# GpSimd's two-operand SBUF work on VectorE, and the float64 shift and weight casts on ScalarE, in a fused attention and mixture-of-experts kernel

## The chip, the cores and the metric

The kernel runs on one core of a Trainium2 chip. The metric is the device time of one execution in microseconds (us). The engines are TensorE (PE; its weight loads are a row of their own, PEld), VectorE (DVE), ScalarE (ACT), GpSimd (POOL) and SyncE (SP). Each engine works through its own queue of instructions in order and waits for other engines by semaphores. A line number such as L750 is a line of the kernel.

## The reference, cut to what matters

Three layers follow each other on 1536 tokens of 512 features. The weights of the middle one, `w_in` and `w_out`, are float64.

```python
# 1: attention, 2 batches x 8 heads, 768 tokens, 64 features: a window of 16 to both sides,
#    and the maxima (keys) and means (values) of each block of 32 tokens
a = softmax(concat([masked q.k / 8, q.kmax / 8 + log(32)]))
x = a @ concat([v, vmean])
# 2: a dense layer, 512 -> 2048 -> 512
h = x @ w_in
x = (h * sigmoid(h)) @ w_out
# 3: 8 experts, 512 -> 1024 -> 512, each token to the one with the largest logit
e = argmax(x @ w_gate);  p = softmax(x @ w_gate)[e]
out = p * (relu(x @ w1[e]) @ w2[e])
```

## The kernel before, in words

Matrix products are made at nearly float32 precision from three products of two parts. A matrix is split into a *high* part, a cast to the matmul type, and a *remainder*, the matrix less its high part. A high part is one copy, a remainder one subtraction of two operands. This splitting is most of what VectorE, ScalarE and GpSimd do.

The tokens go in six chunks of 256. For each chunk and each of four pairs of heads there are scores on PE (`dots`), minima on VectorE (`lows`, L331), exponentials on ScalarE (`exps`), their reciprocal sums on VectorE (`shares`), the normalisation on GpSimd (`norm`, L346), a transpose on PE (`turn`), its copy (`keep`), and the product with the values (`values`), split into `x_high` and `x_rest`. The dense layer goes in eight steps per chunk: `first` (PE, L389), `tanh` (ScalarE), `gated` (VectorE, L402, the scaled product for the sigmoid gate), `g_high` (mostly ScalarE), `g_rest` (mostly GpSimd, L410), and `second` (PE, L426), which runs two steps behind `first`.

The dense weights come as float64 words: 32 blocks of 128 x 512, read as pairs of 32-bit words, low and top. `shrink` (L229) scales the top word's exponent range. `join` shifts the low word down by 29 bits (L233) and joins the top word, moved up by three, to it (L234). `sign_in` (L238) puts the sign back. `high` and `rest` (L256) then split the block. A block's place in SBUF is freed by its remainder, and the next block's load waits for that place.

`route_dots` (L467) makes the router's logits on VectorE, 16 dot products and read-outs a chunk. `route_pick`, `route_rank` and `route_write` put each token into a table by its expert. `plan` and what follows it, chains of small VectorE operations, decide which experts' tiles are worked on in which unit. The first two units come from the first five chunks, the others from all six. A unit loads its expert's weights (SyncE), gathers its tokens (GpSimd's indirect DMA), splits the weights in 16 pieces of 128 x 512 (`split_high`, L151; `split_rest`, L750), and runs both layers (L794 and L819 for a pair of tiles, L831 and L854 for a single tile). `relu_high` and `relu_rest` (L807) split the hidden layer, `scale` and `write` put the result out. The raw weights have one place per half matrix, so the next unit's loads wait for this unit's remainders.

The order of the work is written out by hand up to the first two units. `STEPS` is a table of 1203 short names; each calls the next step of its kind, and so puts its instructions at the end of their engines' queues. A mark behind a name chooses the engine: `'` VectorE, `*` ScalarE, `_` GpSimd; without one the step's own default holds. In it `a` is `shrink`, `b` `join`, `c` `sign_in`, `h` `high`, `p` `rest`, `F` `first`, `t` `tanh`, `u` `gated`, `g` `g_high`, `w` `g_rest`, `G` `second`, `d0` to `d5` one dot product of a chunk, `N0` to `N5` `norm`, `1h` and `2h` `split_high` of the two layers, `1r` and `2r` `split_rest`. The units after that are ordered by `run`, where two strings of 16 letters, `HIGH` and `REST`, say which engine splits which piece: of a unit's 16 remainders ten are VectorE's and six GpSimd's, of its casts 14 ScalarE's and two VectorE's.

Of the kernel before, what the change touches and what calls it, by code (L numbers as in the profile page):

```python
# [13 lines left out]
I64 = mybir.dt.int64  # L14
AF = mybir.ActivationFunctionType
# [6 lines left out]
P = 128  # L22
# [14 lines left out]
G = 4  # L37
# [20 lines left out]
w G D2 G t h_ p b c' u l l l l T2 b a a E2 h g' p p w a_ b F c' t c' F h R2 N2 b u a g q2 l l w p b A2 c' c' b t h h G P2 G a' b l u p p a h C2 g V2 F
b c' c' c' h a h p w p b l q2 l c' t H2 h L2 p b u p h_ A2 F G a a g w l D2 l c' p h t p F F T2 l l u E2 b g' R2 c' N2 h b t w p a P2 t G c' u g a C2'
u w' b h a p' V2 g b c' w' G l l q2 H2 c' h h a L2 F p l t b u b g' p w G D2 c' F A2 T2 h a E2 a t c' b p G h' c' R2 p u h N2 l G p' g b w' c' h' P2  # L60
p' F C2 a b t V2 D2 u c' g H2 h G p T2 E2 a w b F R2 L2 c' N2 h t p G l l u a a g' b w P2 F C2' c' h p' b V2 t F H2 u c' L2 h g p w G t u g w j j J j
# [12 lines left out]
ga rh rr ym 1h 1h 1r yo yo 1h' 1r' 1r' 1h 1r' f1 z 2h 2h 2r' f f lt f f rh rr lc lt lc 1h ls ls ga ga ga ga st 1r' 1h' 1r 1h' 1h 1r z z 1r f1 2r'
# [9 lines left out]
def fused_kernel(ctx: ExitStack, tc, qw, kw, kt, vw, vr, vt, w_in, w_out, w_gate, w1, w2, masks, blocks, items, out):  # L84
# [95 lines left out]
    def block_sums(j):  # L180
        """Sums over the first batch's blocks, on the rows that follow a window's: a column of ones for each block."""
# [22 lines left out]
    def means(b):  # L204
        """The blocks' mean values, on the rows that follow a window's."""
# [20 lines left out]
    def shrink(kind, f, by=nc.scalar):  # L226
        """Float64 words to float32, in place: the exponent's range first, then the bits moved up by three."""
        top = words((kind, f))[1].bitcast(F32)
        (by.mul if by is nc.scalar else by.tensor_scalar_mul)(top, top, TINY)  # L229

    def join(*x):
        low, top = words(x)
        nc.vector.tensor_scalar(low, low, 29, None, op0=ALU.logical_shift_right)  # L233
        nc.vector.scalar_tensor_tensor(low, top, three[:, 0:1], low, op0=ALU.logical_shift_left, op1=ALU.bitwise_or)  # L234

    def sign_in(kind, f, by=nc.gpsimd):
        low, top = words((kind, f))
        by.scalar_tensor_tensor(low, top, sign[:, 0:1], low, op0=ALU.bitwise_and, op1=ALU.bitwise_or)  # L238
# [25 lines left out]
    def rooms(c):  # L264
        """All of a chunk's queries, values and weights, while the places of the dense layers are free."""
# [837 lines left out]
```

## Time and profile before

| | us |
|---|---|
| median of 3 runs | 612.42 |
| the three runs | 605.81, 612.42, 612.69 |
| the profiled execution: span from its first to its last instruction | 605.5 |
| the fastest run, which lies 0.3 us above that span, taken for the profiled execution's own time | 605.81 |
| mean granted TensorE clock of the profiled execution | 0.953 of full speed |

The profile is of one execution. Its view of the busy times says how long each engine had an instruction running, and the windows say the same by stretch, with the granted clock of TensorE as a share of its full speed. In the groups of instructions, two numbers follow the bar: the time in which the group ran, and the mean duration of one in nanoseconds; behind the next bar stands the time in which the engine had been idle just before them, and what ended that. In the view of one line, three durations are given: shortest, median and longest.

### The profile page before, as it was taken

The page shows a single profiled execution, that of the slowest core. Times are in us where ns is not written, and L with a number is a line of the kernel's source. Part 1 is how long each engine was busy: PE and PEld are TensorE (multiplying, and loading weights), DVE is VectorE, ACT ScalarE, POOL GpSimd, SP SyncE. Part 2 cuts the span into 40 slices and gives each one's busy share as a digit, 9 for nine tenths or more (in the row PEclk, how much of TensorE's full clock was granted, in tenths as well). Part 3 has the DMA queues.
Part 4 walks back from the last instruction along what each step waited for, and adds up shares of the span by engine and source line. Part 5 has one row for each costly group of instructions (what it writes and reads, how often), then busy time and mean ns, then how long its engine had stood idle before and what let it go on. Part 6 is the DMA issues. An engine that isn't in the chain of part 4 may idle for free. (4 is left out here: it accounts for less than half of the span.)

```text
span 605.5 us, 9930 instructions
## 1 busy us (share of the span) xinstructions
PE 542.1 (90%) x3554; PEld 467.9 (77%) x3554; DVE 474.4 (78%) x1018; ACT 242.1 (40%) x575; POOL 281.8 (47%) x240
## 2 busy tenths in 40 slices
PE   7878876999999999999899989977799999999883
PEld 3667756778987889788889968866699898988661
DVE  5799999998646788878774586799967487778982
ACT  5764334444324443333332111632243554455531
POOL 2556675453422134252424134894557572454541
PEclk9969988998999999999999999977989999999987
DMA  9996323503377233231210003700056562356540
GB/s 321 327 316 215 104 79 109 187 1 104 117 227 258 70 108 48 81 48 54 79 13 2 36 0 125 260 0 1 1 159 212 184 233 77 97 198 236 185 158 10
DMA packets 40937, 76.24 MB, mean 126 GB/s; under 512 B 3910, under 2 KB 14764, under 8 KB 40882
## 3 DMA queue, kind: packets, MB, share of 16 engines
q1 hardware_dynamic: 35954, 65.81, 34.6%
q0 software_dynamic: 2912, 6.33, 3.1%
q10 hardware_dynamic: 2016, 3.40, 1.6%
q8 instruction: 30, 0.49, 0.4%
q14 instruction: 25, 0.20, 0.1%
HBM read 82.50 MB, written 7.19 MB: 148 GB/s over the span
## 5 line engine op out<-in xcount | busy, mean ns | idle before, releaser
L389 PE MATMUL h<-x,wi 128*128 128x256 f32 x1152 | 151.2, 288 | 5.8 <-DVE t L402 5.1
L426 PE MATMUL x<-wo,g 128*128 128x512 f32 x576 | 148.2, 405 | 5.5 <-POOL g L410 2.2
L389 PEld LDWEIGHTS h<-x,wi 128*128 128x128 f32 x1152 | 144.6, 194 | 8.0 <-issue 4.9
L426 PEld LDWEIGHTS x<-wo,g 128*128 128x128 f32 x576 | 106.2, 191 | 31.6 <-POOL g L410 2.8
L750 POOL TENSOR_TENSOR sp<-r,sp 128x512 fp32r<-128x512 f32 x65 | 88.1, 1387 | 27.2 <-ACT sp L151 22.6
L467 DVE CUSTOM_DVE_ANT_0 dull<-row,gate 128x512 bf16<-128x512 f32 x96 | 92.5, 964 | 3.1 <-DMA gate<-w_gate 1.0
L750 DVE TENSOR_TENSOR sp<-r,sp 128x512 fp32r<-128x512 f32 x79 | 80.5, 1051 | 16.3 <-ACT sp L151 15.8
L410 POOL TENSOR_TENSOR g<-t,g 128x512 fp32r<-128x512 f32 x40 | 58.0, 1455 | 54.4 <-ACT g L151 38.1
L151 ACT CAST sp<-r 128x512 fp32r<-128x512 f32 x123 | 68.8, 624 | 35.4 <-DMA r<-w 16.2
L794 PE MATMUL jh<-xTT,sp 128*128 128x256 f32 x576 | 77.9, 293 | 3.6 <-DVE jT L807 3.6
L794 PEld LDWEIGHTS jh<-xTT,sp 128*128 128x128 f32 x576 | 76.4, 201 | 6.0 <-DVE jT L807 3.9
L819 PE MATMUL jy<-sp,jT 128*128 128x512 f32 x288 | 75.1, 409 | 0.0
L819 PEld LDWEIGHTS jy<-sp,jT 128*128 128x128 f32 x288 | 54.3, 196 | 11.2
L346 POOL TENSOR_TENSOR a<-a,m 128x480 f32<-128x480 f32 x24 | 26.0, 1085 | 71.0 <-DVE m L342 32.4
L337 ACT ACTIVATE a<-a,m 128x120 f32<-128x120 f32 x96 | 36.9, 387 | 54.8 <-DVE m L331 52.5
L399 ACT ACTIVATE t<-h 128x512 f32<-128x512 f32 x48 | 28.5, 596 | 74.7 <-PE h L389 58.0
L402 DVE SCALAR_TENSOR_TENSOR t<-t,h 128x512 f32<-128x512 f32 x48 | 32.7, 682 | 23.7 <-ACT t L399 23.4
L803 ACT ACTIVATE jT<-jh 128x512 fp32r<-128x512 f32 x24 | 14.4, 599 | 61.7 <-PE jh L794 50.1
L863 POOL DMA_INDIRECT out<-y,ids x15 | 16.1, 1074 | 46.4 <-DVE y L859 18.7
L151 ACT CAST g<-t 128x512 fp32r<-128x512 f32 x32 | 19.8, 622 | 35.8 <-DVE t L402 30.8
L513 POOL DMA_INDIRECT tbl<-tb,ix x12 | 14.2, 1180 | 39.5 <-DVE cum L508 16.9
L807 DVE SCALAR_TENSOR_TENSOR jT<-jh,jT 128x512 fp32r<-128x512 f32 x24 | 16.5, 687 | 19.3 <-ACT jT L803 19.3
(181 smaller groups left out, 705.7 us busy)
## 6 DMA issues: line engine op xcount, KB each, us to landing
r<-w SPq DMA_DIRECT2D x36, 1024.0 KB
rawi<-w_in SPq DMA_DIRECT2D x16, 512.0 KB
rawo<-w_out SPq DMA_DIRECT2D x16, 512.0 KB
q<-qw SPq DMA_DIRECT2D x24, 256.0 KB
v<-vw SPq DMA_DIRECT2D x24, 192.0 KB
k<-kw SPq DMA_DIRECT2D x16, 240.0 KB
kt<-kt SPq DMA_DIRECT2D x8, 416.0 KB
x2d<-row ACTq DMA_DIRECT2D x12, 256.0 KB
```

Source lines behind the costliest of these rows:

```text
L151: (nc.scalar.copy if by is nc.scalar else by.tensor_copy)(dst, src)
L337: nc.scalar.activation(a[:, t], a[:, t], AF.Exp, bias=m[:, 0, t:t + 1], scale=-1.0, accum_out=m[:, 1, t:t + 1])
L346: nc.gpsimd.tensor_tensor(a, a, m[:, 2].unsqueeze(2).to_broadcast([P, G, NC]), op=ALU.mult)
L389: nc.tensor.matmul(hs[c, p][:, j], wi[p][:, u, k, j * P:(j + 1) * P], xt[c, k][:, v], start=(j + k + n == 0), stop=(j == 1 and k == KB - 1 ...
L399: nc.scalar.activation(t, hs[c, p], AF.Tanh, scale=0.5)
L402: nc.vector.scalar_tensor_tensor(ts[c, p], ts[c, p], 1.0, hs.pop((c, p)), op0=ALU.add, op1=ALU.mult)
L410: by.tensor_tensor(g[:, 1], ts.pop((c, p)), g[:, 0].bitcast(F32), op=ALU.subtract)
L426: nc.tensor.matmul(x2p[c][i], g[:, v, j, i * P:(i + 1) * P], wo[f][:, u], start=(f == 0 and n == 0), stop=(f == FB - 1 and n == 2))
L467: nc.vector.tensor_tensor_reduce(dull, r, gates[e], 1.0, 0.0, ALU.mult, ALU.add, lg[:, i * E + e:i * E + e + 1])
L750: by.tensor_tensor(dst[:, 1], src, dst[:, 0].bitcast(F32), op=ALU.subtract)
L794: nc.tensor.matmul(hps[i, p][:, j], sp1[p // 2 * 4 + k][:, u, f:f + P], x[v][:, k], start=(k + n == 0), stop=(k == 3 and n == 2))
L819: nc.tensor.matmul(yps[i, t], h[:, v, j, t * P:(t + 1) * P], sp2[2 * p + j][:, u], start=(p + j + n == 0), stop=(p == 3 and j == 1 and n = ...
```

## The change

Five parts:

- `norm`, `rest`, `g_rest` and `split_rest`, all of them operations on two SBUF operands, go from GpSimd to VectorE throughout; so does `sign_in`'s default. The marks in `STEPS` that moved single ones of them to VectorE, or from VectorE and GpSimd elsewhere, go.
- The shift of the low word leaves `join`, on VectorE, for `shrink`, on ScalarE. It reads the upper 16-bit half of the low word, scales it by 2^-13 with an offset that makes the conversion to a whole number round down, and writes 32-bit words.
- `shrink` is always ScalarE's: four were GpSimd's and two VectorE's.
- `high` is always ScalarE's: five were VectorE's or GpSimd's. Three `g_high` of GpSimd go to ScalarE; those of VectorE stay.
- In `run`, all casts go to ScalarE and all remainders to VectorE. The eight casts that `STEPS` marks for VectorE (`1h'`, `2h'`) stay there.

```diff
-    def shrink(kind, f, by=nc.scalar):
-        top = words((kind, f))[1].bitcast(F32)
-        (by.mul if by is nc.scalar else by.tensor_scalar_mul)(top, top, TINY)
+    def shrink(kind, f):
+        low, top = words((kind, f))
+        nc.scalar.mul(top.bitcast(F32), top.bitcast(F32), TINY)
+        half = raws[kind, f].bitcast(U16).rearrange("p (f t) -> p f t", t=4)[:, :, 1]
+        nc.scalar.activation(low, half, AF.Copy, scale=2.0 ** -13, bias=2.0 ** -15 - 0.5)
 
     def join(*x):
         low, top = words(x)
-        nc.vector.tensor_scalar(low, low, 29, None, op0=ALU.logical_shift_right)
         nc.vector.scalar_tensor_tensor(low, top, three[:, 0:1], low, op0=ALU.logical_shift_left, op1=ALU.bitwise_or)
 
-    def sign_in(kind, f, by=nc.gpsimd):
-        low, top = words((kind, f))
-        by.scalar_tensor_tensor(low, top, sign[:, 0:1], low, op0=ALU.bitwise_and, op1=ALU.bitwise_or)
+    def sign_in(*x):
+        low, top = words(x)
+        nc.vector.scalar_tensor_tensor(low, top, sign[:, 0:1], low, op0=ALU.bitwise_and, op1=ALU.bitwise_or)
...
-    def rest(kind, f, by=nc.gpsimd):
+    def rest(kind, f, by=nc.vector):
...
     def norm(c, hp):
         a, m = att[c, hp]
-        nc.gpsimd.tensor_tensor(a, a, m[:, 2].unsqueeze(2).to_broadcast([P, G, NC]), op=ALU.mult)
+        nc.vector.tensor_tensor(a, a, m[:, 2].unsqueeze(2).to_broadcast([P, G, NC]), op=ALU.mult)
...
-    def g_rest(c, p, by=nc.gpsimd):
+    def g_rest(c, p, by=nc.vector):
...
-    HIGH = "aaaaaaadaaaaaaad"
-    REST = "pvvpvvpvpvvpvvpv"
...
-    def split_rest(kind, k, by=nc.gpsimd):
+    def split_rest(kind, k, by=nc.vector):
...
     def split(kind, ks):
         for k in ks:
-            n = 8 * kind + k
-            split_high(kind, k, nc.scalar if HIGH[n] == "a" else nc.vector)
-            split_rest(kind, k, nc.vector if REST[n] == "v" else nc.gpsimd)
+            split_high(kind, k)
+            split_rest(kind, k)
```

Of the table, one line of 23 (the order of the names is the same everywhere, only marks go):

```diff
-t V1 a H1 h' c' u h g p p l X l l b F2 F1 L1 L1 w p b c' F2 F1 F1 F1 b F2 F2 a h t p c' G t h u p b u c' c' g w' l F3 F3 F3 F3 b A2 c' a' a_ h g h a p
+t V1 a H1 h c u h g p p l X l l b F2 F1 L1 L1 w p b c F2 F1 F1 F1 b F2 F2 a h t p c G t h u p b u c c g w l F3 F3 F3 F3 b A2 c a a h g h a p
```

The order of TensorE's and SyncE's instructions does not change. Three places show what moves on VectorE. The first is VectorE's queue in the weight stage, before: `rawi2` and `rawi3` are blocks 2 and 3 of `w_in`, `wi0` is the split form of blocks 0 and 1, `x11` an attention output, `m13` the sums of the exponentials.

```order
L233 TENSOR_SCALAR rawi2_289<-rawi2_289 128x512
L234 SCALAR_TENSOR_TENSOR rawi2_289<-rawi2_289,three_96 128x512
L341 TENSOR_SCALAR m13_437<-m13_437 128x4
L342 RECIPROCAL m13_437<-m13_437 128x4
L256 TENSOR_TENSOR wi0_339<-rawi1_286,wi0_339 128x4x128
L233 TENSOR_SCALAR rawi3_294<-rawi3_294 128x512
L234 SCALAR_TENSOR_TENSOR rawi3_294<-rawi3_294,three_96 128x512
L238 SCALAR_TENSOR_TENSOR rawi2_289<-rawi2_289,sign_94 128x512
L378 TENSOR_TENSOR x11_494<-o11_483,x11_494 128x256
L238 SCALAR_TENSOR_TENSOR rawi3_294<-rawi3_294,sign_94 128x512
```

The same place on VectorE now; `a1` are the attention weights that `norm` scales.

```order
L236 SCALAR_TENSOR_TENSOR rawi2_289<-rawi2_289,three_96 128x512
L343 TENSOR_SCALAR m13_438<-m13_438 128x4
L344 RECIPROCAL m13_438<-m13_438 128x4
L348 TENSOR_TENSOR a1_135<-a1_135,m13_438 128x480
L258 TENSOR_TENSOR wi0_340<-rawi1_286,wi0_340 128x4x128
L236 SCALAR_TENSOR_TENSOR rawi3_295<-rawi3_295,three_96 128x512
L240 SCALAR_TENSOR_TENSOR rawi2_289<-rawi2_289,sign_94 128x512
L380 TENSOR_TENSOR x11_497<-o11_486,x11_497 128x256
L240 SCALAR_TENSOR_TENSOR rawi3_295<-rawi3_295,sign_94 128x512
```

The shifts (L233) are gone from it, and the normalisation (L348) stands in it.

The second is later in the same stage, where VectorE's queue now has places like this one, at the end of the weights (`rawo13`, `rawi14` are blocks of `w_out` and `w_in`, `g15` a split activation):

```order
L258 TENSOR_TENSOR wo12_1352<-rawo12_1211,wo12_1352 128x512
L236 SCALAR_TENSOR_TENSOR rawo13_1213<-rawo13_1213,three_96 128x512
L412 TENSOR_TENSOR g15_1370<-t15_1329,g15_1370 128x512
L240 SCALAR_TENSOR_TENSOR rawo13_1213<-rawo13_1213,sign_94 128x512
L258 TENSOR_TENSOR wo13_1375<-rawo13_1213,wo13_1375 128x512
```

The remainders (L258, L412) were on GpSimd; the last one stands right behind its block's sign (L240), with ScalarE's cast of the block in between on the other engine.

The third place is VectorE's queue at the start of the first routed unit, before: `sp20` to `sp23` are split pieces of the first expert's second matrix, `dull` and `lg5` belong to the last chunk's logits, `jT00` is the first remainder of a hidden quarter.

```order
L151 CAST sp21_3794<-r20_3779 128x512
L467 ISA dull_99,lg5_4038<-row50_4032,gate4_1827 128x512
L467 ISA lg5_4038 128x1
L151 CAST sp22_3795<-r21_3780 128x512
L151 CAST sp23_3796<-r21_3780 128x512
L807 SCALAR_TENSOR_TENSOR jT00_4094<-jh00_4069,jT00_4094 128x512
```

The same place on VectorE now:

```order
L749 TENSOR_TENSOR sp20_3793<-r20_3779,sp20_3793 128x512
L152 CAST sp21_3794<-r20_3779 128x512
L469 ISA dull_99,lg5_4038<-row50_4032,gate4_1827 128x512
L469 ISA lg5_4038 128x1
L749 TENSOR_TENSOR sp20_3793<-r20_3779,sp20_3793 128x512
L749 TENSOR_TENSOR sp21_3794<-r20_3779,sp21_3794 128x512 x2
L152 CAST sp22_3795<-r21_3780 128x512
L749 TENSOR_TENSOR sp22_3795<-r21_3780,sp22_3795 128x512 x2
L749 TENSOR_TENSOR sp23_3796<-r21_3780,sp23_3796 128x512
L152 CAST sp23_3796<-r21_3780 128x512
L749 TENSOR_TENSOR sp23_3796<-r21_3780,sp23_3796 128x512
L805 SCALAR_TENSOR_TENSOR jT00_4094<-jh00_4069,jT00_4094 128x512
```

Eight remainders that were GpSimd's (L749) now stand ahead of the hidden quarter's (L805).

## Rows read from the trace of the kernel before

**Rows 1.** The page's busy times: us (share of the span) and instructions.

```profile
PE 542.1 (90%) x3554; PEld 467.9 (77%) x3554; DVE 474.4 (78%) x1018; ACT 242.1 (40%) x575; POOL 281.8 (47%) x240
```

**Rows 2.** Windows: length; PE, PEld, DVE, ACT, POOL busy us; granted clock; DMA share; GB/s.

```profile
0.00:30.00 30.00, 23.85 (x165) 15.58 (x166) 19.50 (x81) 18.60 (x69) 11.77 (x29) 0.94 0.99 325
30.00:162.00 132.00, 110.91 (x748) 95.34 (x748) 124.35 (x212) 59.59 (x139) 70.96 (x51) 0.91 0.43 136
162.00:388.00 226.00, 217.68 (x1555) 192.07 (x1554) 161.28 (x488) 72.61 (x197) 81.06 (x69) 0.99 0.32 92
388.00:440.00 52.00, 40.12 (x233) 35.99 (x232) 49.97 (x102) 16.98 (x31) 34.95 (x26) 0.86 0.07 24
440.00:540.00 100.00, 100.00 (x646) 90.93 (x645) 70.28 (x87) 46.41 (x85) 54.03 (x45) 0.99 0.50 170
540.00:605.50 65.50, 49.52 (x218) 37.94 (x216) 49.07 (x51) 27.95 (x55) 29.05 (x24) 0.93 0.43 145
```

**Rows 3.** Timeline, PE near 103: start us, us, engine, line, what, idle before.

```profile
103.58 1.20 PE L389 MATMUL h<-x,wi 128*128 128x256 f32 x4 [4.78 <-DVE t L402]
```

**Rows 4.** Groups, shapes apart: busy us, mean ns | idle us before, what ended it.

```profile
L467 DVE CUSTOM_DVE_ANT_0 dull<-row,gate 128x512 bf16<-128x512 f32 x96 | 92.5, 964 | 3.1 <-DMA gate<-w_gate 1.0 <-ACT row L433 0.2
L750 DVE TENSOR_TENSOR sp<-r,sp 128x512 fp32r<-128x512 f32 x79 | 80.5, 1051 | 16.3 <-ACT sp L151 15.8
L750 POOL TENSOR_TENSOR sp<-r,sp 128x512 fp32r<-128x512 f32 x65 | 88.1, 1387 | 27.2 <-ACT sp L151 22.6 <-ACTq L1021 3.4 <-DVE sp L151 1.0
L410 POOL TENSOR_TENSOR g<-t,g 128x512 fp32r<-128x512 f32 x40 | 58.0, 1455 | 54.4 <-ACT g L151 38.1 <-DVE g L151 14.4 <-issue 1.1
L346 POOL TENSOR_TENSOR a<-a,m 128x480 f32<-128x480 f32 x24 | 26.0, 1085 | 71.0 <-DVE m L342 32.4 <-ACT t L399 18.2 <-ACT g L151 9.7
L256 POOL TENSOR_TENSOR wi<-rawi,wi 128x512 fp32r<-128x512 f32 x14 | 21.1, 1515 | 16.7 <-ACT wi L151 11.7 <-DVE wi L151 5.0
L256 POOL TENSOR_TENSOR wo<-rawo,wo 128x512 fp32r<-128x512 f32 x13 | 19.4, 1500 | 23.6 <-ACT wo L151 23.6
```

**Rows 5.** The views of single lines: shortest, median and longest ns, first and last start.

```profile
L750 DVE TENSOR_TENSOR sp<-r,sp x79: 677/691/8139, 379.0 to 594.4; 128x512 fp32r<-128x512 f32 x79
L467 DVE CUSTOM_DVE_ANT_0 dull<-row,gate x96: 659/691/3966, 186.3 to 413.9; 128x512 bf16<-128x512 f32 x96
L402 DVE SCALAR_TENSOR_TENSOR t<-t,h x48: 656/683/690, 46.3 to 378.4; 128x512 f32<-128x512 f32 x48
L233 DVE TENSOR_SCALAR rawo<-rawo x16: 414/423/1544, 43.1 to 157.7; 128x512 int32<-128x512 int32 x16
L234 DVE SCALAR_TENSOR_TENSOR rawo<-rawo,three x16: 751/753/1677, 44.6 to 158.1; 128x512 int32<-128x512 int32 x16
L229 ACT ACTIVATE rawi<-rawi x14: 667/684/712, 22.4 to 146.5; 128x512 f32<-128x512 f32 x14
```

**Rows 6.** Timeline, around the second plan, all engines.

```profile
423.57 5.80 DVE L578 TENSOR_TENSOR til<-til,taken 128x8 f32<-128x8 f32 x1
424.30 5.04 POOL L750 TENSOR_TENSOR sp<-r,sp 128x512 fp32r<-128x512 f32 x4
...
438.34 0.41 PE L662 MATMUL entp<-ident,ents 17*128 17x17 f32 x2 [3.99 <-DMA ents<-tbl,rix]
```

**Rows 7.** Window of line L233 on VectorE alone: length, DVE busy (instructions), clock, DMA.

```profile
0.00:162.00 162.00, 22.34 (x32) 0.92 0.54 171
```

**Rows 8.** Window of line L234 on VectorE alone: length, DVE busy (instructions), clock, DMA.

```profile
0.00:162.00 162.00, 36.27 (x32) 0.92 0.54 171
```

**Rows 9.** Window of line L238 on VectorE alone: length, DVE busy (instructions), clock, DMA.

```profile
0.00:162.00 162.00, 31.32 (x32) 0.92 0.54 171
```

**Rows 10.** Window of line L410 on GpSimd alone: length, POOL busy, clock, DMA.

```profile
30.00:162.00 132.00, 15.40 (x10) 0.91 0.43 136
```

**Rows 11.** Window of line L467 on VectorE alone, read-outs counted in.

```profile
388.00:415.00 27.00, 21.33 (x32) 0.87 0.13 44
```

**Rows 12.** Timeline, PE near 570.

```profile
569.97 1.20 PE L854 MATMUL iy<-sp,hT 128*128 128x512 f32 x4 [2.89 <-POOL sp L750]
```

More of the change, by code (lines that the diff above doesn't have):

```diff
@@ L14 @@
 I64 = mybir.dt.int64
+U16 = mybir.dt.uint16
 AF = mybir.ActivationFunctionType
@@ L58 @@
[L58 to L61, printed above, removed]
@@ L62 @@
-J F t u g w J j J q3 G x F t u g w' G m s m s F t u g w B3 G m m s s D3 T3 E3 R3 N3 q3 O F t d0 u q3 G Y M B3 g' P3 C3 A3 F D3 T3 t E3 R3 N3 w u V3 H3
+P0 v0 l q1 l v1 l A0 a v0 l q1 v0 A0* C0 V0 V0 a C0 q1 l H0 A0_ A0 b c L0 H0 T1 L0 h E1 D1 P0 A1 C0' R1 T1 v1 q2 l l v1 v1 l l V0 D1 V0 H0 a E1 H0
+L0 A1 T1 N1 p P1 D1 R1 C1 b T1 L0 N1 E1 E1 P1 V1 C1' A1_ H1 a a R1 c N1 A1_ L1 P1 V1 h C1 H1 b R1 a N1 p F0 F0 F0 V1 P1 b c L1 c b a h a F0 H1 C1
+t V1 a H1 h c u h g p p l X l l b F2 F1 L1 L1 w p b c F2 F1 F1 F1 b F2 F2 a h t p c G t h u p b u c c g w l F3 F3 F3 F3 b A2 c a a h g h a p
@@ new lines @@
+w G D2 G t h p b c u l l l l T2 b a a E2 h g' p p w a b F c t c F h R2 N2 b u a g q2 l l w p b A2 c c b t h h G P2 G a b l u p p a h C2 g V2 F
+b c c c h a h p w p b l q2 l c t H2 h L2 p b u p h A2 F G a a g w l D2 l c p h t p F F T2 l l u E2 b g' R2 c N2 h b t w p a P2 t G c u g a C2'
+u w b h a p V2 g b c w G l l q2 H2 c h h a L2 F p l t b u b g' p w G D2 c F A2 T2 h a E2 a t c b p G h c R2 p u h N2 l G p g b w c h P2
+p F C2 a b t V2 D2 u c g H2 h G p T2 E2 a w b F R2 L2 c N2 h t p G l l u a a g' b w P2 F C2' c h p b V2 t F H2 u c L2 h g p w G t u g w j j J j
@@ L69 @@
-u g' w G x d4 d4 d4 d4 F t d4 d4 d4 d4 u d4 d4 d4 g w w d4 d4 d4 d4 d4 F G t u g_ w F G i t u g r e e G plan tiles F F read prow f1 f1 t u w' G ids ga
-ga f2 f2 F G t u g w t 1h g u g w G lt lt 1h 1r' 1h w lc ls 1r' lc ls 1h 1r 1h 1h 1r 1h 1h' 1r 1r 1r' 1r' f1 G G x d5 d5 ga ga f1 d5 d5 2h 2r 2h 2h'
+w B4 G D4 T4 E4 R4 e F t A4* g q5 d2 u d2 d2 N4 w g G P4 C4' d2 d2 F t u V4 H4 B5 d2 L4 d2 d2 d2 g w w G D5 T5 E5 R5 N5 F t d2 d2 u q5 G P5 A5_ C5'
+d2 g' i F t u V5 H5 w L5 g B5 G D5 r e x T5 E5 d3 R5 N5 F t u d3 g' w w q5 d3 d3 G e P5 C5' A5 d3 F t u V5 g H5 d3 L5 w B5 d3 G D5 T5 E5 R5 N5 F t u
@@ L71 @@
+d3 g w q5 G P5 C5 d3 d3 A5 d3 d3 F d3 d3 t d3 u V5 H5 g w B5 L5 d3 G D5 i T5 E5 R5 N5 F t A5 u G r P5 C5 F g' w e t V5 H5 L5 u g w G e F t u g' G F t
+u g' w G x d4 d4 d4 d4 F t d4 d4 d4 d4 u d4 d4 d4 g w w d4 d4 d4 d4 d4 F G t u g w F G i t u g r e e G plan tiles F F read prow f1 f1 t u w G ids ga
+ga f2 f2 F G t u g w t 1h g u g w G lt lt 1h 1r 1h w lc ls 1r lc ls 1h 1r 1h 1h 1r 1h 1h' 1r 1r 1r 1r f1 G G x d5 d5 ga ga f1 d5 d5 2h 2r 2h 2h'
 d5 2r 2r 2h 2r 2h' f2 2r 2h 2r 2h 2r 2h' 2r f2 f f f f rh rr d5 d5 d5 f f lt f f d5 rh rr d5 d5 d5 d5 d5 d5 d5 i lc ls 1h 1r 1h 1r 1h 1r 1h 1r f f f z
-lt f f rh rr lc ls z 2h 2r 2h f f f rh z r z e 2r e 2h 2r' 2h' rr 2r 1h 1r' 1h 1h 1h 1r 1r f f f cn f pl 1r' pl pl pl rh rr pl pl pl pl pl pl pl pl pl
@@ L73 @@
-pl pl pl pl pl pl pl pl pl pl pl pl z z 2h 2r f f 2h f f rh rd ex 2r' ex ex ex ex rr ex ex ex ex f1 f2 f1 z z 2h 2r' ym* 2h 2r f2 f f z it f f ic ga
-ga rh rr ym 1h 1h 1r yo yo 1h' 1r' 1r' 1h 1r' f1 z 2h 2h 2r' f f lt f f rh rr lc lt lc 1h ls ls ga ga ga ga st 1r' 1h' 1r 1h' 1h 1r z z 1r f1 2r'
+lt f f rh rr lc ls z 2h 2r 2h f f f rh z r z e 2r e 2h 2r 2h' rr 2r 1h 1r 1h 1h 1h 1r 1r f f f cn f pl 1r pl pl pl rh rr pl pl pl pl pl pl pl pl pl
+pl pl pl pl pl pl pl pl pl pl pl pl z z 2h 2r f f 2h f f rh rd ex 2r ex ex ex ex rr ex ex ex ex f1 f2 f1 z z 2h 2r ym* 2h 2r f2 f f z it f f ic ga
@@ L75 @@
+ga rh rr ym 1h 1h 1r yo yo 1h' 1r 1r 1h 1r f1 z 2h 2h 2r f f lt f f rh rr lc lt lc 1h ls ls ga ga ga ga st 1r 1h' 1r 1h' 1h 1r z z 1r f1 2r
 """
```

8 lines of the change are left out of this document (2 added, 6 removed).

## The prediction

> **What bounds the kernel now.** I read the page's busy times first. TensorE (PE) is busy 542.1 of 605.5 us, VectorE (DVE) 474.4, GpSimd (POOL) 281.8 [rows 1]. A whole-span share hides the stages, so next come the windows, cut where the kind of work changes [rows 2]. The reader is to see three kinds of stage. From 440 to 540 us PE is busy 100.00 of 100.00 us: nothing off PE can shorten that. From 162 to 388 PE has 217.68 of 226.00: at most 8.3 us to win. From 30 to 162, and from 388 to 440, DVE is busy 124.35 of 132.00 and 49.97 of 52.00 while PE has 110.91 and 40.12, at a granted clock of 0.91 and 0.86: there VectorE sets the pace, PE waits for it, and part of PE's time is at the lower of its two levels (1.2 instead of 2.4 GHz). PE's longest wait there, 4.78 us before 103.58, is for VectorE's gated product (L402) [rows 3]. The last stretch, 540 to 605.5, has PE at 49.52 with neither engine full.
>
> Then I asked what VectorE's time is made of. The same subtraction (L750) takes VectorE 677 ns at its fastest and 691 at the median, and 8139 at the longest; its mean is 1051 [rows 4, 5]. The routing's dot product (L467) has a median of 691 and a mean of 964. The timeline shows what the long ones have in common: an operation on 8 elements a partition (L578) took 5.80 us from 423.57, and four GpSimd subtractions filled 424.30 to 429.34 [rows 6]. The gated product, which reads a PSUM bank, never took over 690 ns [rows 5]. So VectorE's operations on SBUF alone stand still while GpSimd works on two SBUF operands, and a large part of "DVE busy" in the tight stages is that.
>
> As to how much PE could give: taken at its busy time, 605.5 - 542.1 = 63 us. The Trainium skill's page "Perfetto Trace Analysis" (Identifying the Most-Contended Engine) says matmul busy time is no good measure of the distance to the limit and asks for the weight loads' share; by [rows 1, 2] the loads fill 90.93 of 100 us where PE never waits and 467.9 in all, so PE would need about 515 us, and the ceiling would be 90 us. The sum stays far under either.
>
> **The change, part by part.**
>
> *Work that leaves VectorE.* The 32 shifts (L233) go to ScalarE: 32 x 0.423 (their undisturbed median, [rows 5]) = 13.5 us, of a recorded 22.34 [rows 7]. VectorE's casts of routed weights go too, but for eight that the step table marks.
>
> *Work that comes to VectorE.* GpSimd's 27 weight remainders (L256), 40 activation remainders (L410), 24 normalisations (L346) and 65 routed remainders (L750) [rows 4]. VectorE's price for such a subtraction is 0.69 us [rows 5], against 1.39 to 1.52 on GpSimd; for the 480-element normalisation I estimate 0.65 by length. Sum: 132 x 0.69 + 24 x 0.65 = 106.7 us.
>
> *The stalls that go.* Mean less median, times count: L467 96 x 0.273 = 26.2 us, L750 79 x 0.360 = 28.4 us. For the shift, the join (L234) and the sign (L238): 22.34 - 13.5 = 8.8, 36.27 - 32 x 0.753 = 12.2, 31.32 - 32 x 0.75 = 7.3 [rows 5] and [rows 7 to 9] (the sign taken at the join's median, being the same form). With L578 that is 88 us in the groups shown. GpSimd keeps copies, memsets and indirect DMAs alone, so I take this as gone. Bounds: nothing of it is cured if something else holds VectorE (0), all 88 if not; I take all, as the 677 and the 8139 ns are the same instruction.
>
> So VectorE gives up about 88 + 13 and takes on 107: its total hardly moves. What moves is where: stage by stage.
>
> *30 to 162 us.* 124.4 - 28.3 (stalls of the three word operations) - 13.5 + 27 x 0.69 + 10 x 0.69 (10 of the 40 L410 lie here, [rows 10]) + 7 x 0.65 (seven of the normalisations, the second chunk's last three and the third's four, by the step table) = 112.7 us. VectorE works in order, so a remainder now waits in its queue for ScalarE's cast, and what stands behind it (signs, joins, the next gated product, on which PE's first layer waits) waits with it. By the order of instructions nine places have no other work, or one short operation, between the producer and the remainder; each costs a pass of ScalarE, 0.684 at L229's price [rows 5], 0.7 with the hand-over, so 6.3 us. That makes 119. PE needs 110.91 at the clock it had, so it does not stop this. 132 to 120: 12 us. Bounds: 0 (the waits eat it) and 20 (no waits, stalls gone).
>
> *ScalarE in that stretch.* It has 59.59 us busy of 132. It gets 32 shifts and six exponent scalings at 0.684 (price of the same strided form, L229, [rows 5]) and five casts: about 29 us, so 89 of 120. That is hidden as long as ScalarE is not late for the join. What a shift costs on a strided 16-bit view is not in the trace; from below VectorE's 0.42, from above GpSimd's two-operand price, 1.5 [rows 4]; I take the ScalarE row, the nearest in form. At 1.5 the 32 would fill another 26 us of ScalarE, which would then be full and VectorE late for it.
>
> *162 to 388 us.* VectorE takes on 30 x 0.69 + 12 x 0.65 + 4 x 0.69 = 31 us and sheds stalls of about the same size (most of L467's). The second layer's products run two steps behind the first's, so a remainder has two of PE's steps before it is asked for; by the step table one of 48 lacks that distance. I take 1 us of the 8.3, bounds -5 and 6.
>
> *388 to 440 us.* The 16 dot products and their read-outs hold VectorE 21.33 us to 415 [rows 11]; undisturbed 16 x 0.77 = 12.3, so 9.0 go, and 5.6 of L578 (0.2 left, an estimate for 8 elements). But some 20 remainders come, 13.8 us, eight of them ahead of the first remainder of a hidden quarter, for which PE waits. Casts and small stalls give another 4 to 6. The chain from the last logits to the gather of the second plan's rows, where PE waited 3.99 us at 438.34 [rows 6], comes out 5 us earlier. Bounds 1 and 9.
>
> *440 to 540 us.* Nothing, as PE is full; VectorE has 70.28 of 100 and loses stalls.
>
> *540 to the end.* PE waited 2.89 us for a GpSimd remainder at 569.97 [rows 12]. Those remainders also release the raw weights for the next load, so the loads move up. I take 4 us, bounds 0 and 8.
>
> *Sum.* 12 + 1 + 5 + 4 = 22 us. The profiled execution has a span of 605.5; the fastest of the three runs, 605.81, lies 0.3 above that, and I take it for the execution's own time. The median is 612.42. So 605.8 - 22 = 583.8 against that execution; I add 3.3, half of the 6.6 us by which the median lies above it, here and in the rivals, as the runs after will scatter alike: 587 us.
>
> **The rivals.**
>
> *The large gain.* VectorE's stretch falls to its 112.7 us, PE waits less and is granted the full clock for longer (0.91 and 0.86 in [rows 2]). Then 20 + 5 + 8 + 6 = 39 us: 605.8 - 39 + 3.3 = 570. For it: PE's need at full clock is well below 110.91. Against: in-order queues on three engines seldom meet without waits.
>
> *PE was the bound all along.* VectorE's stalls lay in its spare time; only the 5 of the second plan and a little elsewhere show: 605.8 - 5 + 3.3 = 604. For it: PE at 90%. Against: the stretch from 30 to 162 in [rows 2].
>
> *VectorE inherits GpSimd's waits (slower).* GpSimd stood 23.6 and 11.7 us in front of weight remainders for ScalarE's casts, and 38.1 in front of activation remainders [rows 4]. If VectorE serves all of the first two and a quarter of the third in the weight stretch, it has 112.7 + 35.3 + 9.5 = 157.5 us there instead of 132. 25 lost, 4 won at the end and none in the second plan, as the remainders stand ahead there too: 605.8 + 25 - 4 + 3.3 = 630. It decides once the inherited waits pass 132 - 112.7 = 19 us. Against: GpSimd came early and waited; VectorE comes later to the same place, with other work before it. The Trainium skill's "ScalarE: Activation LUTs" (Rules for kernel authors) speaks for this rival: it puts multiplications and additions on VectorE, not ScalarE, and the shift moves the other way; the rows here agree with it on the price, 0.42 against 0.68 [rows 5].
>
> *The change does not free VectorE.* GpSimd's remaining copies and DMA issues still hold it. Its 13 copies and 44 indirect DMAs at about 1 us would leave some 10 of the 88 us: within the forecast's range.
>
> **How the numbers follow.** Forecast 0.63, by itself 575 to 600; large gain 0.16; PE the bound 0.14; inherited waits 0.07. The range's low end is where every stretch reaches its upper bound, 20 + 6 + 9 + 8 = 43 us, so 566; its high end, 606, is PE the bound with 3 us won instead of 5. It leaves out some 0.15. Two per cent, about what a measurement of this kernel can tell, is 12.2 us: faster means below 600.2. Forecast 0.60 of its 0.63 and all of the large gain: 0.76 faster. The rest of the forecast and PE the bound: 0.17 within. Inherited waits: 0.07 slower.
>
> **What would show it.** Right: L750 and L467 on VectorE with mean and median both near 0.69 and no operation over 2 us; 30 to 162's work done near 150 us; the plan's products on PE some 17 us earlier than 438.34 in all (12 + 1 + 5, within a few); POOL busy under 60 us. ScalarE's shifts at 0.68. Wrong: VectorE idle before remainders, ended by ScalarE's casts, of more than 19 us in the weight stretch; shifts over 1 us; L467 still slow, which would put the stalls on something other than GpSimd's two-operand work.

## The result and the profile after

The changed kernel takes 584.42 us (median of 4 runs, 582.64 to 585.12), the kernel before, with one more run beside it, 609.88 us (605.81 to 612.69): ratio 0.958, 95% interval 0.952 to 0.964. It is faster, and close to the 587 us that were forecast. A second set of 6 runs gave 581.89 us (579.32 to 585.62), so differences of 2 or 3 us between single sets are not read below.

The page of the changed kernel (engine, busy us, share of the 583.0 us span, instructions) answers to [rows 1]:

```profile
PE 532.1 (91%) x3554; PEld 465.1 (80%) x3554; DVE 428.9 (74%) x1124; ACT 273.7 (47%) x634; POOL 58.7 (10%) x75
```

VectorE (DVE) has 45.5 us less, although GpSimd (POOL) handed it 156 operations. The durations by source line (ns: min/median/max) answer to [rows 5]; L749, L469 and L232 are the routed remainder, the dot product and ScalarE's new shift:

```profile
L749 DVE TENSOR_TENSOR sp<-r,sp x144: 677/684/719, 372.4 to 570.8; 128x512 fp32r<-128x512 f32 x144
...
L469 DVE CUSTOM_DVE_ANT_0 dull<-row,gate x96: 661/691/980, 173.5 to 400.4; 128x512 bf16<-128x512 f32 x96
...
L232 ACT ACTIVATE rawi<-rawi x16: 646/664/782, 21.3 to 134.8; 128x512 int32<-128x512 uint16 x16
```

The longest remainder fell from 8139 to 719 ns, the longest dot product from 3966 to 980: the stalls are gone. No operation of VectorE takes over 1.48 us now.

To see where the time went, I cut both traces at the same work, not at the same times. TensorE (PE) issues the same products in the same order in both kernels, so the start of a given product is a landmark: the first product of the dense layer; its 337th; the first plan's count (`cnt`); the first routed product (`jh`); the second plan's transpose (`entp`); the last first-layer product of a pair of tiles (the last `jh`); the end. Each stage in us, worked out from the profiles:

```
kernel                      start weights dense plan1 plan2 routed  tail   span
before                       39.3  113.2  210.9  24.4  50.5  101.5  65.6  605.5
changed                      43.8   94.8  211.5  31.8  42.3  102.8  56.0  583.0
difference                   +4.5  -18.4   +0.6  +7.4  -8.2   +1.3  -9.6  -22.5
e1 routed remainders back    44.9   94.4  209.2  31.8  49.9  102.8  61.2  594.2
e2 normalisation back        37.5   93.6  211.4  32.4  42.3  102.8  55.2  575.3
e3 shift back                45.2  102.5  211.0  30.3  41.8  101.5  56.0  588.2
e4 other remainders back     42.9   98.6  209.7  31.5  42.3  102.6  55.8  583.5
b1 useless two operands      44.1   94.7  209.3  32.0  60.3  102.7  62.9  605.9
b2 useless one operand       43.9   95.4  213.0  30.7  53.4  101.6  59.1  597.2
b3 load behind the gather    45.1   94.4  211.7  26.1  42.3  101.5  55.8  577.0
b4 before, shift alone       38.7   95.8  209.0  31.7  50.4  102.5  65.0  593.0
c0 changed, again            43.8   94.3  209.2  31.8  42.1  101.6  55.8  578.5
c1 e2 and b3 together        38.4   92.9  210.1  26.5  42.2  102.6  55.2  567.9
c2 c1, later transpose       38.4   93.7  212.1  26.1  42.0   99.7  55.3  567.3
c3 two casts in 16 back      44.5   94.7  209.4  31.7  41.8  101.6  55.9  579.5
```

A stage that an edit doesn't touch lies within about 2.5 us of the changed kernel's, mostly within 1. So three stages gain 36 us, two lose 12, and the two where PE is nearly full lose 2.

The stages as windows, before and after (the first column is the stretch; then its length, busy us of each engine, granted clock, DMA share, GB/s):

```profile
39.30:152.50 113.20, 96.30 (x625) 82.72 (x624) 108.39 (x170) 49.42 (x109) 63.77 (x44) 0.92 0.39 126
...
363.40:387.90 24.50, 24.25 (x145) 21.07 (x145) 16.05 (x46) 8.66 (x16) 15.36 (x15) 0.99 0.52 187
387.90:438.30 50.40, 38.56 (x225) 34.46 (x223) 48.88 (x96) 16.98 (x31) 34.76 (x25) 0.86 0.08 25
```

```profile
43.80:138.60 94.80, 89.63 (x625) 79.12 (x624) 83.73 (x174) 67.62 (x144) 0.50 (x1) 0.98 0.40 130
...
350.20:382.00 31.80, 25.93 (x145) 22.80 (x145) 16.45 (x53) 8.74 (x16) 8.62 (x11) 0.89 0.51 166
382.00:424.30 42.30, 34.40 (x226) 31.03 (x224) 40.68 (x119) 16.83 (x31) 3.92 (x3) 0.96 0.05 14
```

Columns three to seven are PE, its loads, DVE, ACT, POOL. In the weight stage VectorE filled 108.4 of 113.2 us before; now PE has 89.6 of 94.8 and VectorE 83.7, so PE is now the fuller engine there. In the second plan VectorE is still the fuller engine, 40.7 of 42.3 us, but with 8.2 us less. In the first plan PE idled 0.25 us before and 5.87 now.

### The profile page after: what moved, and what is told of

Read it like the earlier page. It is cut to its first block, busy times and chain, and to the rows that moved or that the text cites. A ratio compares the mean times of both kernels' runs of the same rounds, so it can differ in the third digit from the quotient of the medians.

```text
span 583.0 us, 9792 instructions
## 1 busy us (share of the span) xinstructions
PE 532.1 (91%) x3554; PEld 465.1 (80%) x3554; DVE 428.9 (74%) x1124; ACT 273.7 (47%) x634; POOL 58.7 (10%) x75
## 5 line engine op out<-in xcount | busy, mean ns | idle before, releaser
L428 PE MATMUL x<-wo,g 128*128 128x512 f32 x576 | 144.2, 399 | 1.7 <-DVE wo L258 1.4
L428 PEld LDWEIGHTS x<-wo,g 128*128 128x128 f32 x576 | 104.7, 188 | 25.6 <-DVE wo L258 2.0
L749 DVE TENSOR_TENSOR sp<-r,sp 128x512 fp32r<-128x512 f32 x144 | 91.6, 685 | 9.9 <-ACT sp L152 9.7
L152 ACT CAST sp<-r 128x512 fp32r<-128x512 f32 x136 | 75.6, 624 | 15.2 <-PE jy L817 13.9
L792 PEld LDWEIGHTS jh<-xTT,sp 128*128 128x128 f32 x576 | 75.0, 198 | 6.9 <-DVE jT L805 4.6
L469 DVE CUSTOM_DVE_ANT_0 dull<-row,gate 128x512 bf16<-128x512 f32 x96 | 66.3, 691 | 2.0
L412 DVE TENSOR_TENSOR g<-t,g 128x512 fp32r<-128x512 f32 x48 | 32.7, 687 | 7.3 <-ACT g L152 7.1
L805 DVE SCALAR_TENSOR_TENSOR jT<-jh,jT 128x512 fp32r<-128x512 f32 x24 | 16.5, 689 | 26.9 <-ACT jT L801 26.8
L152 ACT CAST g<-t 128x512 fp32r<-128x512 f32 x35 | 21.7, 624 | 30.7 <-DVE t L404 27.7
L333 DVE CUSTOM_DVE_ANT_0 a<-s,mask 128x120 f32<-128x120 f32 x96 | 21.3, 277 | 13.8 <-PE s L314 13.7
L354 PE MATMUL t<-ident,a 128*120 128x128 f32 x96 | 16.1, 295 | 8.0 <-DVE a L348 7.4
```

The source lines that it names most:

```text
L152: (nc.scalar.copy if by is nc.scalar else by.tensor_copy)(dst, src)
L333: nc.vector.tensor_tensor_reduce(a[:, t], ps[:, t, :NC], mask[:, v], -0.125, 3.0e38, ALU.add, ALU.min, m[:, 0, t:t + 1])
L412: by.tensor_tensor(g[:, 1], ts.pop((c, p)), g[:, 0].bitcast(F32), op=ALU.subtract)
L428: nc.tensor.matmul(x2p[c][i], g[:, v, j, i * P:(i + 1) * P], wo[f][:, u], start=(f == 0 and n == 0), stop=(f == FB - 1 and n == 2))
L469: nc.vector.tensor_tensor_reduce(dull, r, gates[e], 1.0, 0.0, ALU.mult, ALU.add, lg[:, i * E + e:i * E + e + 1])
L749: by.tensor_tensor(dst[:, 1], src, dst[:, 0].bitcast(F32), op=ALU.subtract)
```

## The experiments

My theory was the forecast's: VectorE's operations on SBUF stand still while GpSimd works on two SBUF operands, and their removal is the gain. The rivals: GpSimd was slow itself, in chains that others waited for; or the move of the shift is the gain.

**One part undone at a time.** Four kernels, each the changed one but for one edit.

e1: the 65 routed remainders back on GpSimd, by the old table and marks:

```
-    def split_rest(kind, k, by=nc.vector):
+    def split_rest(kind, k, by=nc.gpsimd):
...
-            split_rest(kind, k)
+            split_rest(kind, k, nc.vector if REST[n] == "v" else nc.gpsimd)
```

> Only the 65 routed remainders go back to GpSimd, all else as in the changed kernel. Theory (VectorE's operations on SBUF alone stand still while GpSimd works on two SBUF operands): the dot products' mean, 0.691 us in the changed kernel, goes back to 0.85 to 1.0, some routed remainder on VectorE takes over 2 us, the stretch of the second plan (382 to 427 us) grows by about 7 us and the tail after 527 by about 9: some 600 us, 594 to 604. Rival (the gain came from the weight stretch alone, the routed stage is TensorE's): 584 to 588, with the dot products slow but nobody waiting.

Measured 596.12 us (592.87 to 596.96). The second plan takes 49.9 us again (+7.6) and the tail 61.2 (+5.2); no other stage is longer by more than 1.1. The tail's loss is less than the 9 us that I expected. Its timeline at the second plan (start, us, engine, line):

```profile
416.10 5.83 DVE L586 TENSOR_TENSOR cmp<-til,itc 128x48 f32<-128x48 f32 x1
...
416.82 5.03 POOL L751 TENSOR_TENSOR sp<-r,sp 128x512 fp32r<-128x512 f32 x4
...
421.85 0.68 DVE L808 SCALAR_TENSOR_TENSOR jT<-jh,jT 128x512 fp32r<-128x512 f32 x1
```

A 48-element operation, 0.21 us in the changed kernel, ends 0.08 us behind the fourth GpSimd subtraction. The pattern of [rows 6] is back with one edit.

e2: the 24 normalisations back on GpSimd:

```
-        nc.vector.tensor_tensor(a, a, m[:, 2].unsqueeze(2).to_broadcast([P, G, NC]), op=ALU.mult)
+        nc.gpsimd.tensor_tensor(a, a, m[:, 2].unsqueeze(2).to_broadcast([P, G, NC]), op=ALU.mult)
```

> Only the 24 normalisations go back to GpSimd. Theory (in the first 45 us the normalisation stands in VectorE's queue behind the minima, and TensorE waits 0.5, 2.3, 2.1 and 1.3 us for it; on GpSimd it ran beside them): the first product of the first layer comes at 39 to 40.5 us instead of 43.8, and the whole at 579 to 582. Rival (GpSimd's normalisation holds VectorE up as much as it frees it): 583.5 to 588, the first product near 43 to 44.

Measured 576.81 us (568.69 to 578.28), faster than the changed kernel and than I expected. The start falls by 6.3 us, to 37.5. PE's waits before the transposes of the normalised scores, in the changed kernel and in e2 (us in total, times, longest):

```profile
PE t L354 <- DVE a L348: 7.4, 6, 2.3
```

```profile
PE t L354 <- POOL a L348: 4.0, 4, 1.9
```

So the normalisation's move cost time: on VectorE it stands in the queue behind the next heads' minima. Within the start these waits are 6.5 and 3.3 us, half of the gain. The other half is PE's own busy time, 30.36 and 26.65 us at a granted clock of 0.82 and 0.92, and that part differs between runs: 29.59 us at 0.90 in c1, a later kernel with the same edit.

e3: the shift back on VectorE, ahead of the join:

```
-        nc.scalar.activation(low, half, AF.Copy, scale=2.0 ** -13, bias=2.0 ** -15 - 0.5)
...
+        nc.vector.tensor_scalar(low, low, 29, None, op0=ALU.logical_shift_right)
```

> Only the 32 shifts go back to VectorE, which does them at 0.42 us instead of ScalarE's 0.68. Theory (VectorE is the fuller engine of the weight stretch, 91 of 105 us, so 13.5 us more there is partly on the path): 588 to 595, VectorE at 105 of 110 us in that stretch. Rival (with the stalls gone VectorE has room for the shifts, and ScalarE's shift only lengthens the way to the join and holds the copies behind it): 579 to 585.

Measured 590.14 us (589.67 to 593.21). The weight stage takes 102.5 us, 7.7 more, with VectorE at 95.6 us:

```profile
45.20:147.60 102.40, 92.02 (x625) 80.01 (x624) 95.61 (x203) 55.13 (x119) 0.50 (x1) 0.97 0.36 120
```

e4: weight and activation remainders back on GpSimd, with their old marks:

```
-    def rest(kind, f, by=nc.vector):
+    def rest(kind, f, by=nc.gpsimd):
...
-    def g_rest(c, p, by=nc.vector):
+    def g_rest(c, p, by=nc.gpsimd):
```

> Only the weight remainders (27) and the activation remainders (40) go back to GpSimd. Theory (stalls): join and sign, 0.75 us each in the changed kernel, go to means of 0.9 or more, the weight stretch grows by about 8 to 12 us of the 15 it won, and the whole comes to 590 to 598. Rival (what was won there comes from the shift's move and the shorter way, not from stalls): 582 to 587, although join and sign are slow again.

Measured 585.15 us (582.67 to 586.19): no difference, the rival's number. The stalls did come back; the sign (L240), at most 754 ns in the changed kernel, by source line:

```profile
L240 DVE SCALAR_TENSOR_TENSOR rawi<-rawi,sign x16: 723/749/1764, 24.9 to 139.1; 128x512 int32<-128x512 int32 x16
L240 DVE SCALAR_TENSOR_TENSOR rawo<-rawo,sign x16: 741/970/1865, 46.5 to 149.0; 128x512 int32<-128x512 int32 x16
```

But VectorE was rid of 67 subtractions in exchange: the weight stage is 3.8 us longer; start and dense layers are 2.7 shorter, which is no more than their scatter. In the whole time, stalls and work are worth about the same here.

**The shift alone.** b4 is the kernel before with the shifts and exponent scalings moved to ScalarE, and all two-operand work left on GpSimd:

```
+        nc.scalar.activation(low, half, AF.Copy, scale=2.0 ** -13, bias=2.0 ** -15 - 0.5)
...
-        nc.vector.tensor_scalar(low, low, 29, None, op0=ALU.logical_shift_right)
```

> The kernel before, with nothing but the 32 shifts and the exponent scalings moved to ScalarE; all two-operand work stays on GpSimd. Theory (VectorE's work and stalls together set the pace of the weight stretch, and the shift takes 13.5 us and more of stalls from it): the weight stretch is 7 to 13 us shorter, 594 to 603 where the kernel before has 606 to 613 (ratio 0.975 to 0.99). Rival (the stalls alone set the pace, or ScalarE comes late): ratio 0.995 to 1.01.

Measured 595.30 us (591.57 to 596.40), ratio 0.974 (0.965 to 0.982): more than half of the change's gain. The weight stage takes 95.8 us, 17.4 less than in the kernel before, where the whole change took off 18.4; I had expected 7 to 13:

```profile
38.70:134.60 95.90, 91.93 (x628) 81.11 (x625) 88.63 (x139) 66.33 (x140) 60.26 (x41) 0.95 0.47 153
```

VectorE has 88.63 us instead of 108.39. The difference, 19.8, is just what the 27 shifts of this stage took in the kernel before, work and stall together (19.63); joins and signs are no faster than before. PE now fills 91.9 of 95.9 us, so a faster VectorE could win little more, which fits e4's small loss.

That doesn't make the rest of the change worthless. e3 is the other half of the comparison: it has all of the change but the shift (the exponent scalings are ScalarE's in e3 and b4 alike), and its weight stage is 10.7 us shorter than in the kernel before. The shift is worth 17.4 us there when it comes first and 7.7 when it comes last, the rest 10.7 and 1.0: the two gains overlap.

**Useless work on GpSimd.** Is it GpSimd's slowness in a chain or what it does to VectorE? In b1 and b2 VectorE does every remainder, and at the 65 old places GpSimd does work that nobody reads:

```
+        if by is nc.gpsimd:
+            nc.gpsimd.tensor_tensor(spare[1], spare[0], dst[:, 0, :HP * NC].bitcast(F32), op=ALU.subtract)
```

> The changed kernel, with VectorE doing every remainder; at the 65 places where GpSimd did a routed remainder before, GpSimd also subtracts a cast weight from a spare tile into another spare tile (128x480, two SBUF operands), and nobody reads it. Theory (two SBUF operands on GpSimd hold VectorE up, whatever they are for): some routed remainder or dot product on VectorE takes over 2 us, the dot products' mean goes to 0.8 or more, and the whole comes to 592 to 603, at least as slow as with the remainders themselves on GpSimd (596). Rival (GpSimd's own slowness in the chain was what cost): nobody waits for these, so 583 to 588.

Measured 607.93 us (606.85 to 611.29), 0.997 (0.993 to 1.001) of the kernel before: useless work eats the whole gain, and more than the 592 to 603 that I expected. Second plan +18 us, tail +7. PE's longest wait there is for VectorE's remainder of a hidden quarter (us in total, times, longest), 14.0 us where the changed kernel has 4.4:

```profile
PE jh L799 <- DVE jT L812: 14.3, 2, 14.0
```

Groups by line (busy us, mean ns):

```profile
L753 DVE TENSOR_TENSOR sp<-r,sp 128x512 fp32r<-128x512 f32 x144 | 135.9, 995 | 0.5 <-ACT sp L152 0.4
...
L755 POOL TENSOR_TENSOR spare<-spare,sp 128x480 f32<-128x480 f32 x65 | 94.3, 1451 | 33.2 <-ACT sp L152 27.9 <-DVE sp L152 2.1
```

b2 puts two copies, of one SBUF operand each, in the subtraction's place:

```
+            for _ in range(2):
+                nc.gpsimd.tensor_copy(spare[1], dst[:, 0, :HP * NC].bitcast(F32))
```

> The same, but at each of the 65 places GpSimd makes two copies of a cast weight into the spare tile (128x480, one SBUF operand each) instead of the subtraction, about as long in all (the cast of 128x512 on GpSimd took 0.63 us). Theory (it takes two SBUF operands): VectorE's dot products and remainders stay at 0.69 us in the mean and the whole at 583 to 588. Rival (any work of GpSimd on SBUF holds VectorE): as slow as the run with two operands, 592 to 603.

Measured 597.99 us (597.27 to 599.01): my theory's 583 to 588 is refuted, though the copies do less than the subtractions. The same groups:

```profile
L753 DVE TENSOR_TENSOR sp<-r,sp 128x512 fp32r<-128x512 f32 x144 | 116.0, 855 | 3.9 <-ACT sp L152 2.5 <-PE jy L825 1.2
...
L756 POOL COPY spare<-sp 128x480 f32<-128x480 f32 x130 | 107.5, 827 | 25.0 <-ACT sp L152 17.6 <-DVE sp L152 0.8
```

So it doesn't take two operands on GpSimd's side. VectorE's remainder, with two operands in SBUF, is held by copies too: 0.17 us each in the mean (855 against 685), against 0.31 beside the subtractions. The useless work also reads the split tile, so the tile's next cast might have waited for it, but that isn't what cost: no wait of another engine ended with it in b1, and 0.6 us did in b2. The Trainium skill's page "SBUF — State Buffer" (Who interferes with whom) puts it this way: a VectorE instruction with two SBUF inputs contends with a GpSimd instruction that reads SBUF. These two runs agree; my "two SBUF operands" was too narrow.

**The first plan.** In the changed kernel TensorE waits 5.87 us for a gather of a few table rows. The timeline, kernel before first, then the changed kernel, then with the weight loads made to wait for the gather (b3):

```profile
366.08 2.23 DVE L600 TENSOR_SCALAR ends<-ends 128x8 f32<-128x8 f32 x1
...
370.22 1.00 POOL L653 DMA_INDIRECT ents<-tbl,rix  x1 [1.93 <-DVE ei L554]
...
371.96 1.06 SPq L722 DMA_DIRECT2D r<-w  x2
...
372.56 0.37 PE L662 MATMUL entp<-ident,ents 4*128 4x4 f32 x2 [0.25 <-DMA ents<-tbl,rix]
```

```profile
350.18 0.18 PE L529 MATMUL cnt<-cum,ones 128*128 128x8 bf16 x1
...
357.12 1.06 SPq L724 DMA_DIRECT2D r<-w  x2
...
358.70 0.99 POOL L655 DMA_INDIRECT ents<-tbl,rix  x1 [1.86 <-DVE g L412]
...
364.78 0.37 PE L664 MATMUL entp<-ident,ents 4*128 4x4 f32 x2 [5.87 <-DMA ents<-tbl,rix]
```

```profile
351.20 0.18 PE L529 MATMUL cnt<-cum,ones 128*128 128x8 bf16 x1
...
359.74 0.99 POOL L655 DMA_INDIRECT ents<-tbl,rix  x1 [1.96 <-DVE g L412]
...
362.01 1.06 SPq L724 DMA_DIRECT2D r<-w  x2
362.02 0.37 PE L664 MATMUL entp<-ident,ents 4*128 4x4 f32 x2 [2.08 <-DMA ents<-tbl,rix]
```

```
+    def bring1(i, g):
+        fetch1(i, g, got0[0] if i == 0 else None)
```

> The changed kernel, with the first unit's first-layer weights (two loads of 1 MB) made to wait for the first plan's gather of table rows. Theory (in the changed kernel these loads are issued at 357.1, 1.6 us ahead of that gather, which then takes 6.1 us instead of 2.3 to reach TensorE): the wait before the plan's transpose falls from 5.9 to under 2.5 us, and the whole comes to 579 to 582.5. Rival (the gather is slow without them too): the wait stays over 4.5 us and the whole at 583 to 587.

Measured 579.09 us (577.99 to 579.74). From the gather's issue to the transpose it takes 2.28 us, and 6.08 with two loads of 1 MB issued 1.6 us ahead of it. In the kernel before the order was gather, 370.22, then loads, 371.96, and 2.34 us. Counted from the first plan's count, the loads come 1.6 us earlier in the changed kernel (6.94 behind it, 8.52 before) and the gather 1.7 us later (8.52 and 6.78). The loads wait for the plan's arithmetic, in which the 8-element L600 had taken 2.23 us beside four memsets of GpSimd; the gather waits for the table's last write, starts 3.9 us behind the end of that write's issue in both kernels, and the write comes later against the count. So the loads came to overtake it.

It isn't the two-operand work's leaving GpSimd that did this. b4, which keeps all of that work there, has the long stage too (31.7 us), with the loads 0.50 us ahead of the gather. In e4, where the arithmetic is held as long as before (L560 2.08 us beside the memsets), they are 0.47 us ahead. The gather then takes 5.8 us in both. In e3 they are 0.26 us ahead: the order hangs on tenths of a microsecond.

**Together.** c1 is e2's edit and b3's in one kernel, c2 moreover turns the second plan's table twelve products later, and c3 asks for the rest of the tail:

> The changed kernel again, as it is, beside the three that follow on the same chip: 582 to 587, as before.

> The changed kernel with the two edits that gained, together: normalisations on GpSimd, and the first routed weights behind the first plan's gather. If they are independent, 7.6 and 5.3 us add up: 568 to 574. Rival (the normalisations' gain ran into the same collision, so part of it is counted twice): 575 to 579.

Measured 571.72 us (569.19 to 573.98) beside 581.89 for the changed kernel on the same chip. Start and first plan gain 5.4 and 5.3 us: the two edits add up.

```
- ... f2 f f z it f f ic ga
+ ... f2 f f z f f it ic ga
```

> The same, and the second plan's transpose, before which TensorE waits 3.5 us for its gather in the changed kernel, put behind the next twelve products of the first layer (3 us). Theory (TensorE is full from there on, so what it doesn't wait it keeps): 2 to 3 us less than the run without, the wait under 1 us. Rival (the rows of the next unit are gathered that much later, and TensorE waits before their transposes instead): within 1 us of it.

Measured 568.72 us (566.96 to 571.28), ratio to the kernel before 0.933 (0.927 to 0.938). The medians' 3.0 us against c1 are within the two sets' scatter; second plan and routed stage together are 3.1 us shorter. The wait before the transpose is 1.87 us, not under 1, and another of 0.93 comes up behind it, for the rows of the next unit. c2 beats the kernel before and the changed one.

```
-            split_high(kind, k)
+            split_high(kind, k, nc.scalar if HIGH[8 * kind + k] == "a" else nc.vector)
```

> The changed kernel, with only the casts of every eighth routed weight back on VectorE, as the table of the kernel before had it (two of sixteen). With the routed remainders back on GpSimd the tail after 527 us lost 5.2 us, in the kernel with the shift alone, which has these casts on VectorE too, 9.0. Theory (such a cast cost time only while it stood still under GpSimd's subtractions): 583 to 587, each cast 0.42 us. Rival (VectorE is the wrong engine for them anyway): 587 to 590.

Measured 584.16 us (581.28 to 586.77), the tail 55.9. VectorE's casts of routed weights in b4, with GpSimd's subtractions beside them, and in c3 without:

```profile
L152 DVE CAST sp<-r 128x512 fp32r<-128x512 f32 x21 | 24.7, 1185 | 0.0
```

```profile
L152 DVE CAST sp<-r 128x512 fp32r<-128x512 f32 x21 | 9.3, 445 | 0.0
```

The casts cost nothing by themselves. The tail's 65.0 us in b4 against 61.2 in e1, 3.8 us, fits casts that stand still under subtractions.

## Why the prediction was right

The total was: 22 us forecast against the profiled execution, 22.5 found between the two spans (25.5 between the medians). The way to it named the places of the gains and missed those of the losses, most sizes were off, and the errors cancelled: the three gains were 15 us larger than the sum had them, and losses of 14 us that it didn't have took that back. That the total came so close is luck. The start of the sum was off too: in every run whose span is on record the time lies 1.7 to 2.2 us above the span, so the profiled execution took some 607.4 us and not 605.81, which moves the forecast by less than 1 us.

- **The stalls go: right**, and that they are GpSimd's doing is shown by e1 and b1. The condition, two SBUF operands on GpSimd, was too narrow (b2). "VectorE's total hardly moves" was wrong: it fell by 45.5 us. Of the signs that the prediction named, VectorE's durations, GpSimd's 58.7 us and the shift's 0.66 came; the second plan's transpose came 14.0 us earlier, not 17. The operations that VectorE takes on cost what was priced (remainders 0.69, normalisation 0.67), but the 88 us of stalls left out the casts of routed weights and the plain copies.
- **30 to 162 us, 12 forecast, 18.4 found.** The sum made VectorE 11.7 us lighter (-28.3 - 13.5 + 30.1); in the weight stage it is 24.7 lighter (108.39 to 83.73). Two terms were mis-sized, both worked out from the trace with overlaps counted once: the added work is 23.5 us (4 normalisations, not 7, and a remainder behind another operation takes only 0.62 us more), and copies and small operations that I hadn't listed gave back another 6. "PE needs 110.91 at the clock it had" failed too: the clock rose from 0.92 to 0.98 and PE's busy time fell by 6.7 us, which the sum had left to the large gain. And the text spoke of stalls as the mechanism here. By the sum's own terms the shift with its stalls was worth 22.3 us and all the rest -10.6. Alone, the shift gave 17.4 (b4), and the rest didn't lose but gained 10.7 (e3). ScalarE's pass at 0.68 was right (0.66 to 0.67). VectorE waited 4.9 us for ScalarE's casts where I had 6.3, and 2.5 us for its shifts, for which I had nothing. What these waits cost by themselves no run shows; PE is the fuller engine now.
- **The start, left out of the sum, lost 4.5 us.** The step that failed is the normalisations' price: 0.65 us of work each, and no wait. PE's transposes need them, and in VectorE's queue they stand behind the next minima. I asked that question for the remainders and not for them.
- **162 to 388 us, +1 forecast (bounds -5 and 6), some 8 lost: wrong, outside the bounds.** The dense layers moved by 0.6; the first plan lost 7.4, 5.7 of it by b3 to the loads that overtook the gather. I had written that loads move up only for the tail, as a gain.
- **388 to 440, 5 forecast (1 to 9), 8.2 found; 440 to 540, nothing forecast, 1.3 lost: right.** e1 gives 7.6 of the 8.2 to the remainders.
- **The tail, 4 forecast (0 to 8), 9.6 found, above the bounds.** Before, PE waited 2.89 us for a GpSimd remainder [rows 12] and another 2.85 for one of VectorE's, which I hadn't counted; both waits went. e1 puts 5.2 us on the remainders; e1 against b4 leaves some 4 that fit the held casts, for which I had no term.
- **Rivals.** Inherited waits came to 4.9 of the 19 us from which they would decide. The large gain is near what c2 reaches, by three edits that undo side effects. That PE was the bound all along is refuted by b4; that it is the bound now, in the weight stage, fits e4's small loss.

## What to carry to other kernels

On an in-order engine count, stage by stage, work plus stall of each operation, and ask which engine bounds the stage once it is taken away. In the weight stage one operation moved to a third engine with room won 17.4 us by itself, all the other moves 10.7, and both together 18.4: behind the first relief the next engine is nearly full, and the second is worth little. An operation on the way to the busiest engine is priced by what stands ahead of it in its new queue, not by its length. After a speed-up, look which transfers now start earlier than a small one that somebody waits for.

## What was unexpected of the hardware

GpSimd's one-operand copies hold VectorE's two-operand operations too (855 against 685 ns in the mean), and take longer beside them: 582 ns at the fastest, 827 in the mean. In the kernel before, e1 and b4 an operation of VectorE stood still through four to six GpSimd subtractions in a row (5.8 to 8.1 us); in b1, with as many subtractions and runs of up to six of them, none took over 2.22 us. One difference stands in the traces. In those three kernels GpSimd's next subtraction in a row starts 13 to 84 ns before the last one ends; in b1, where all of them write one spare tile, it starts 78 or 79 ns after. And every remainder or dot product of VectorE that took over 2 us in the kernel before, e1, e4 and b4 ended 0.55 to 0.56 us after the end of a GpSimd operation that no other overlapped there. That isn't the whole condition: beside eleven overlapping subtractions in e1, dot products (1.64 to 1.67 us) and subtractions (1.72) took turns.

GpSimd need not read anything: L600 (2.23 us before) and L560 (2.08 in e4), on 8 and 2 elements, ended within 0.03 us of the end of four memsets. Operations that read PSUM were free of it: the gated product (48 in each run) and the hidden layer's remainder never took over 0.70 us in any run.
